# First six units' inverse as 64x64 tiles: a fused delta-rule attention and MLP kernel, with a new order

## The chip, the cores and the metric

One NeuronCore of a Trainium2 chip runs the whole kernel. The metric is device time in microseconds (us). PE is the matrix engine, DVE the vector engine, ACT the scalar engine, POOL GpSimd, and SP issues most of the DMAs.

## The reference

For 4 batches and 8 heads (32 heads in all) of 768 tokens and 48 dimensions, a delta rule runs over the tokens with a 48 x 48 state per head; its outputs, 384 wide per token, go through an MLP with the tanh form of GELU.

```python
k_n = k / (np.linalg.norm(k, axis=-1, keepdims=True) + 1e-06)
for t in range(S):
    y[:, :, t] = np.einsum('bhd,bhde->bhe', q[:, :, t], state)
    v_old = np.einsum('bhde,bhd->bhe', state, kt)
    state = state + bt[:, :, :, None] * np.einsum('bhd,bhe->bhde', kt, vt - v_old)
...
h = x @ w_in                                  # 3072 x 384 by 384 x 2048
g = 0.5 * h * (1.0 + np.tanh(c * (h + 0.044715 * h * h * h)))
return g @ w_out                              # 3072 x 2048 by 2048 x 384
```

## The kernel before, in words

The 768 tokens are cut into 12 chunks of 64. A chunk has two units (u = 2c and 2c + 1); a unit holds 16 heads as 8 pairs, with the tokens of one head of a pair on partitions 0 to 63 and of the other on 64 to 127. Within a chunk the rule is a triangular system, so each unit inverts a 64 x 64 unit triangular matrix per head, and a state is carried from chunk to chunk.

The steps of a chunk, by the names in the order text:

- k, q, v: loads (L468, mostly on SP). sq, sum, pow, eps, inv: the norms of k. kn, qb, vb: scaled k, and q and v in bf16.
- T (or Tk, Tq): transposes of k and q on PE, evicted by kT; for some units a DMA transpose, turn, takes their place. G (GD, GQ): the products k k and k q, evicted to dn and wq.
- F, lp, x0, L, and xm1, xa1 to xm6, xa6: the inverse of the 8 x 8 diagonal blocks, a recurrence on DVE for both units of the chunk together. xb: times beta. xe: spread over the blocks into zt.
- KZ, kz, GM, lw: the keys times zt, their products, and a masked copy of these into lw, which holds two 64 x 64 parts per head.
- X10, X11, then A4, rt4, B4 and A5, rt5, B5: two doubling steps of the block inverse, in the tile bd. bd is block-diagonal: 128 x 128 per pair, the two heads' 64 x 64 matrices on its diagonal and zeros elsewhere. A product's result lies 64 wide for both heads, so bringing it back into bd takes two evictions on ACT or DVE, bde0 (upper half) and bde1 (all rows, the upper ones times zero), or one eviction xi and two copies bdc0, bdc1 on POOL or DVE.
- V, K, R, U, Un, Q, O, On, S, Sn: the chunk's right-hand side, the product with bd (U), outputs (On) and the new state (Sn).
- X, xT (or turnx, a DMA transpose): the outputs turned for the MLP. up0 to up15, gelu0 to gelu3, down00 to down13, Z0, Z1, out: the MLP and its stores.

Nothing is scheduled while it runs. `ORDER` lists all steps; a step stands in the queue of the engine behind its colon (a, d, g, s for ACT, DVE, POOL, SP; PE without one), and `@` names its first PSUM bank. Each engine works through its queue in order and waits at semaphores that `Flow.emit` derives from buffers and banks. Weights come by POOL's DMA queue in four parts (w1.0, w1.1, w2.0, w2.1); `fill` steps are matmuls on zeros that nothing reads.

Of the kernel before, what the change touches and what calls it, by code (L numbers as in the profile page):

```python
# [17 lines left out]
ident:d tmplz:d tmpl0:g one:g blk1:g tmpl1:g triwq4:g pad4:d wz:d bdz5:d blk2:g ident2:g bdz4:g k0x0.11:s k0x1.10:s k0x0.10:a k0x0.00:a k0x0.01:a  # L18
k1.11:s k0x1.11:s k0x1.00:a k0x1.01:a k1.01:s k1.00:s k1.10:s beta01:a tabS:a beta00:a blk3:g pad5:d ladj5.0:d pad1:d mmlw:d bdz2:d identf:d two:d
rowz:d rows1:g mln0:g sq.0a:g triwq1:d unit:d bdz3:d ladj4.1:d own:d triwq2:d pad0:d sel:d ladj5.1:d sum.0a:d mwp0:g half:g pow.0a:a trilw2:d trilw3:d  # L20
eps.0a:d inv.0a:d mmuq:d bdz1:g sq.0b:g k2.11:s k2.10:s k2.00:s beta11:a beta10:a kn.0:g fill0@0 fill1@0 fill2@0 fill3@0 fill4@0 fill5@0 fill6@0
fill7@0 Tk.0@0 betaT0@1 sum.0b:d bdz0:d first1:d pow.0b:a eps.0b:d inv.0b:d kn.1:d Tk.1@2 sq.1:a sum.1:d kTk.0:a pow.1:a GD.0@4 kTk.1:d GD.1@2
betaT1@0 k2.01:s dn.0:a dn.1:a sq.2:a F.0@2 betaN011:d eps.1:d pad3:d betaN010:d inv.1:d pad2:d betaN000:d betaN001:d kn.2:d kn.3:d sum.2:d Tk.2@3
q0.01:s q2.00:s q0.00:s q0.10:s q0.11:s v0.00:s q2.10:s q2.11:s v0.10:s q2.01:s v0.11:s k3.10:s k3.01:s v2.10:s v0.01:s lp.0:d betaH0:d L.0@2 x0.0:d
betaL0:d xm1.0:d betaN101:d xa1.0:d betaN110:d xm2.0:d betaN100:d xa2.0:d xm3.0:d xa3.0:d betaN111:d xm4.0:d Tk.3@1 trilw1:a triwq0:a kTk.2:a GD.2@4
# [8 lines left out]
bde50.0:a bde51.0:a GM.2@2 w2.0:g pow.3:g eps.3:g xa2.2:d lw.2:d X11.2:g xm3.2:d X10.2:d xa3.2:d xm4.2:d inv.3:d xa4.2:d triwq3:d xm5.2:d xa5.2:d
xm6.2:d Tq.2@4 U.0@0 qb.3:a kTq.2:a X10.3:g X11.3:g Un.0:a GQ.2@4 Tq.3@7 kTq.3:a O.0@0 On.0:a S.0@2 A4.2@7 Sn.0:a rt4.2:d xa6.2:d X.0@0 xb.2:g xe.5:g
wq.2:d xT.0:a B4.2@7 GQ.3@2 A4.3@6 up8.0@0 up9.0 xe.4:d rt4.3:d tabG:a xi4.2:a KZ.4@4 kz.4:d B4.3@6 up10.0 up11.0 GM.4@4 wq.3:d lw.4:d X11.4:d
bde40.3:a bde41.3:a gelu2.0:a up4.0@2 up5.0 up6.0 up7.0 bdc41.2:g bdc40.2:g kn.6:g vb.3:g A5.3@0 up0.0@4 A5.2@1 up1.0 rt5.3:d vb.2:d rt5.2:d KZ.5@0
B5.3@6 gelu1.0:a sq.4:a xi5.3:a V.1@2 B5.2@1 K.1 X10.4:d kz.5:d GM.5@6 bde50.2:a R.1:a sum.4:d qb.7:g kn.7:g qb.6:g bdc51.3:g k5.00:s q4.11:s q4.01:s
q4.00:s k5.10:s q4.10:s k5.01:s q5.00:s up2.0 up3.0 A4.4@0 bdc50.3:g lw.5:d rt4.4:d turn.7:s bde51.2:a gelu0.0:a sq.5:d up12.0@2 up13.0 up14.0 U.1@6
qb.8:g B4.4@4 up15.0 down00.0@5 bde40.4:a gelu3.0:a qb.9:a Un.1:d X10.5:d pow.4:g Q.1@0 S.1@6 O.1 G.7@2 dn.7:a wqa.7:a On.1:a bde41.4:a X11.5:g  # L40
eps.4:g sum.5:d inv.4:d kn.9:d Sn.1:d kn.8:g wqb.5:g down01.0 down02.0 A4.5@2 T.9@3 turn.6:s G.6@0 X.1@6 rt4.5:d kT.9:d dn.6:a B4.5@4 T.8@7 xT.1:d
kT.8:d wq.6:d G.9@2 bde40.5:a v3.01:s v2.01:s vb.5:g vb.4:g v4.00:s q5.10:s v3.00:s q6.10:s k6.01:s q7.10:s v3.10:s k6.10:s k6.11:s v4.10:s k6.00:s
v4.01:s k7.00:s k7.01:s k7.11:s k7.10:s q6.01:s q7.11:s down03.0 bde41.5:a A5.5@4 dn.9:a wq.9:d qb.10:g Z0.0:a F.3@7 A5.4@6 V.2@0 rt5.5:d lp.3:d
rt5.4:d G.8@2 K.2 L.3@7 up12.1@4 up13.1 up14.1 B5.4@6 up15.1 dn.8:a R.2:a wqa.8:a bde50.4:a bde51.4:a F.4@2 B5.5@3 bde50.5:a bde51.5:a gelu3.1:a
x0.3:d xm1.3:d xa1.3:d xm2.3:d xa2.3:d xm3.3:d xa3.3:d xm4.3:d xa4.3:d xm5.3:d pow.5:g lp.4:d up8.1@0 up9.1 up10.1 L.4@6 up11.1 xa5.3:d xm6.3:d
eps.5:d xa6.3:d x0.4:d xb.3:g xm1.4:d xa1.4:d inv.5:d xm2.4:d xa2.4:d xm3.4:d xa3.4:d xm4.4:d xa4.4:d xm5.4:d xe.7:d xe.6:g qb.11:g U.2@2 Un.2:a
down10.0@7 down11.0 gelu2.1:a Q.2@2 S.2@4 KZ.6@0 down12.0 xa5.4:d Sn.2:d xm6.4:d xa6.4:d xb.4:d xe.9:d xe.8:d O.2 kz.6:a sq.6:a On.2:a GM.6@0 up0.1@4
up1.1 up2.1 KZ.7@6 up3.1 up4.1@2 up5.1 kz.7:a KZ.9@6 up6.1 up7.1 lw.6:d kn.11:d gelu0.1:a kz.9:d GM.7@4 lw.7:d kn.10:g wqb.8:g X11.6:g X10.6:g
gelu1.1:a turn.10:s X10.7:g X11.7:g T.11@0 KZ.8@6 down13.0 GM.9@2 G.10@4 kT.11:a G.11@0 Z1.0:d kz.8:a dn.10:a wqa.10:a dn.11:a wqa.11:a sum.6:d A4.6@7
down10.1@6 down11.1 rt4.6:d lw.9:d v3.11:s q6.11:s turnx.2:s k8.11:s k8.10:s q7.01:s A4.7@7 B4.6@4 bde40.6:a rt4.7:d vb.7:d bde41.6:d down12.1 F.5@2  # L50
lp.5:d B4.7@7 GM.8@0 A5.6@4 down00.1@5 down01.1 lw.8:d pow.6:g wqb.7:g bde40.7:a bde41.7:a vb.6:a sq.7:a q8.10:s v5.11:s k8.00:s k8.01:s v4.11:s
q7.00:s L.5@7 A5.7@0 V.3@2 rt5.6:d x0.5:d xm1.5:d B5.6@4 K.3 X10.9:g X11.9:g eps.6:d rt5.7:d xa1.5:d A4.9@0 sum.7:d wqb.11:g X10.8:g X11.8:g sq.8:g
bde50.6:a bde51.6:a R.3:a B5.7@1 bde50.7:a bde51.7:a down02.1 down13.1 down03.1 up0.2@2 xm2.5:d xa2.5:d xm3.5:d xa3.5:d rt4.9:d xm4.5:d Z1.1:d xa4.5:d
xm5.5:d Z0.1:d xa5.5:d xm6.5:d inv.6:d xa6.5:d xb.5:g U.3@0 vb.9:a Un.3:a A4.8@6 up1.2 up2.2 Q.3@4 rt4.8:d S.3@0 O.3 up3.2 up4.2@6 up5.2 up6.2 xe.11:d
Sn.3:d B4.9@0 kn.13:d On.3:a gelu0.2:a bde40.9:a bde41.9:a xe.10:g up12.2@4 B4.8@1 KZ.11@2 out11.0:s v5.01:s q6.00:s qb.13:d bde40.8:d v6.00:s
out00.0:s q8.00:s turnx.3:s up7.2 KZ.10@3 up13.2 up14.2 up15.2 A5.9@0 kz.11:a gelu1.2:a kz.10:d bde41.8:a rt5.9:d GM.10@2 GM.11@6 lw.10:d kn.12:g
pow.7:g qb.12:g X11.10:g eps.7:g lw.11:d turn.13:s vb.8:a gelu3.2:a up8.2@0 up9.2 up10.2 up11.2 up0.3@4 A5.8@2 up1.3 up2.3 up3.3 gelu2.2:a B5.9@3
X10.10:d A4.10@0 V.4@6 gelu0.3:a rt5.8:d B5.8@2 K.4 G.13@4 rt4.10:d R.4:d B4.10@0 down10.2@1 down11.2 X10.11:g wqb.10:g X11.11:g bde50.8:a bde51.8:d
turn.12:s k9.01:s sum.8:d bde50.9:a bde51.9:a dn.13:a wq.13:d inv.7:d xi4.10:d bdc40.10:g bdc41.10:g U.4@2 Un.4:a down12.2 down13.2 A4.11@2 rt4.11:d
G.12@4 Q.4@6 Z1.2:a dn.12:a S.4@0 Sn.4:d wq.12:d O.4 k9.00:s v5.10:s v5.00:s On.4:a qb.15:g k9.10:s v7.01:s v7.11:s v6.01:s k9.11:s v7.10:s q8.01:s  # L60
q8.11:s down00.2@2 F.6@3 B4.11@6 A5.10@7 up8.3@4 up9.3 lp.6:d rt5.10:d x0.6:d L.6@3 xm1.6:d xa1.6:d xm2.6:d xa2.6:d kn.15:d up10.3 down01.2 pow.8:g
# [798 lines left out]
```

## Time and profile before

| | |
|---|---|
| median of 3 runs | 263.66 us (261.0 to 264.15) |
| the profiled execution | 262.76 us, its span 261.0 us |
| mean granted PE clock | 0.928 |
| busy: PE, DVE, ACT, POOL | 236.6, 191.2, 169.5, 135.7 us |
| MLP matmuls | 576 (L780) and 384 (L791) |
| product matmuls of the inverse (L660) | 768 |

The span runs from the first to the last instruction. Busy times are unions of an engine's instructions; an engine that is busy is not always at its peak. The granted clock is the share of full speed that PE was given.

### The profile page before, as it was taken

The numbers are of one execution on the slowest core, as the hardware profiler recorded it, in microseconds if no ns is written. First come the engines' busy times: TensorE is split into PE (matmuls) and PEld (weight loads), VectorE is DVE, ScalarE is ACT, GpSimd is POOL, SyncE is SP. The second block draws the span as 40 slices with busy tenths as digits, with TensorE's granted clock in tenths as the row PEclk, the third lists the DMA queues.
The fourth block names the chain that finished last, engine by engine and source line by source line (L and its number), as shares of the span: only waits on it lengthen the run. The fifth ranks groups of instructions, "written<-read, shape, count | busy, mean of one in ns | idle before, by whom it ended". The sixth has DMA issues, their size and how long they took to land.

```text
span 261.0 us, 11939 instructions
## 1 busy us (share of the span) xinstructions
PE 236.6 (91%) x5320; PEld 182.3 (70%) x5320; DVE 191.2 (73%) x444; ACT 169.5 (65%) x261; POOL 135.7 (52%) x172
## 2 busy tenths in 40 slices
PE   5188688976999999999999998999999999999994
...
PEclk9655755699999999999999999999999999999999
...
GB/s 97 162 173 197 123 148 199 127 128 141 133 114 144 124 153 57 122 125 110 162 119 140 108 36 118 159 37 135 130 76 3 4 154 32 31 36 48 45 93 60
DMA packets 104019, 28.10 MB, mean 108 GB/s; under 512 B 98080, under 2 KB 103200, under 8 KB 103968
## 3 DMA queue, kind: packets, MB, share of 16 engines
q1 hardware_dynamic: 98736, 23.56, 51.4%
...
## 4 chain that ended last, share of the span: by engine, by line
PE 62%; DVE 12%; DMA 10%; SPq 6%; POOL 4%; ACT 3%; issue 2%; POOLq 0%
PE ps L780 20%; PE ps L791 20%; DMA qraw<-in_q_dram 8%; SPq L468 6%; PE ps L660 6%; DVE lw L600 2%; PE ps L597 2%; PE ps L586 2%; PE ps L708 2%; PE ps L546 2%; DMA kraw<-in_k_dram 2%; PE ps L610 1%; PE ps L729 1%; PE ps L522 1%; PE ps L715 1%
## 5 line engine op out<-in xcount | busy, mean ns | idle before, releaser
L780 PE MATMUL ps<-xT,W 128*128 128x256 bf16 x576 | 75.6, 274 | 1.6 <-issue 0.8
L791 PE MATMUL ps<-W,gT 128*128 128x384 bf16 x384 | 72.3, 326 | 0.0
L784 ACT ACTIVATE gT<-ps 128x1024 bf16<-128x1024 f32 x48 | 48.3, 1020 | 22.0 <-PE ps L780 21.7
L780 PEld LDWEIGHTS ps<-xT,W 128*128 128x128 bf16 x576 | 51.7, 98 | 10.7 <-issue 1.2
L791 PEld LDWEIGHTS ps<-W,gT 128*128 128x128 bf16 x384 | 34.1, 97 | 18.6
L678 POOL COPY bd<-xi 64x256 f32<-64x256 f32 x28 | 11.0, 398 | 49.3 <-ACT xi L341 43.5
L600 DVE CAST_PREDICATED lw<-mlw,ps 128x1024 bf16<-128x1024 uint16 x24 | 29.1, 1218 | 7.6 <-PE ps L597 7.4
L650 POOL TENSOR_SCALAR_AFFINE_SELECT bd<-lw 64x512 bf16<-64x512 bf16 x33 | 22.3, 678 | 21.4 <-DVE lw L600 16.0
L494 POOL TENSOR_TENSOR nrm<-nrm,half 128x16 f32<-128x16 f32 x10 | 29.4, 2943 | 4.5 <-DVE nrm L492 4.3
L666 DVE TENSOR_TENSOR rl<-ps,two 128x384 bf16<-128x384 f32 (+1 forms) x48 | 22.8, 486 | 10.6 <-PE ps L660 10.4
L660 PE MATMUL ps<-rl,bd 128*128 128x64 bf16 x384 | 19.5, 198 | 0.7 <-DVE rl L666 0.7
L344 ACT ACTIVATE bd<-ps,low 128x512 bf16<-128x512 f32 x27 | 18.3, 677 | 2.3 <-DVE bd L341 2.3
L341 ACT ACTIVATE bd<-ps 64x512 bf16<-64x512 f32 x27 | 15.7, 585 | 5.9 <-PE ps L660 5.7
L632 DVE TENSOR_TENSOR ps<-ps,xl 128x96 f32<-128x96 f32 (+2 forms) x72 | 16.0, 223 | 4.0 <-PE ps L626 2.1
L660 PEld LDWEIGHTS ps<-rl,bd 128*128 128x128 bf16 x384 | 16.4, 101 | 3.1 <-DVE rl L666 0.9
L522 PE MATMUL ps<-ident,tok 128*128 128x128 bf16 x96 | 10.1, 256 | 8.9 <-POOL tok L513 6.7
L341 DVE COPY ob<-ps 128x384 f32<-128x384 f32 x7 | 3.9, 551 | 19.0 <-PE ps L791 19.0
L660 PEld LDWEIGHTS ps<-lw,bd 128*128 128x128 bf16 x384 | 15.1, 98 | 3.7 <-ACT bd L344 0.5
L635 DVE TENSOR_TENSOR xl<-ps,xl 128x96 bf16<-128x96 f32 (+2 forms) x72 | 16.2, 225 | 1.8
L660 PE MATMUL ps<-lw,bd 128*128 128x32 bf16 (+1 forms) x384 | 17.1, 183 | 0.3 <-ACT bd L344 0.3
L513 POOL TENSOR_TENSOR tok<-kraw,nrm 128x384 bf16<-128x384 f32 x16 | 14.6, 914 | 3.3 <-DVE xl L635 1.1
L341 ACT ACTIVATE dn<-ps 128x512 bf16<-128x512 f32 x20 | 11.9, 594 | 5.7 <-PE ps L546 5.5
...
## 6 DMA issues: line engine op xcount, KB each, us to landing
...
W<-in_moe_w_in_dram POOLq DMA_DIRECT2D x2, 768.0 KB, 10.5
W<-in_moe_w_out_dram POOLq DMA_DIRECT2D x2, 768.0 KB, 10.8
...
kT<-tok SPq DMA_TRANSPOSE x12, 3.3
```

What stands on the lines that cost most here:

```text
L341: return e.activation(out, in_, ACT.Copy) if e is nc.scalar else e.tensor_copy(out, in_)
L344: return e.activation(out, in_, ACT.Copy, scale=by) if e is nc.scalar else e.tensor_scalar(out, in_, by, None, op0=ALU.mult)
L494: if e is nc.scalar else e.tensor_tensor(nr[:, 1, hx], nr[:, 0, hx], half[:, hx], ALU.pow), reads=[nrn, "half"] + ["one"] * (c < ROOTS),
L600: A(("dve",), op("lw"), lambda e, P: e.copy_predicated(lw[m][:, :, :, :].rearrange("p h w t -> p h (w t)"), mlw[:, :, :].rearrange("p w t ...
L632: A(("dve",), f"xm{m}.{c}", lambda e, P, m=m, w=w, part=part: e.tensor_tensor(part(P), P(f"L.{c}")[:, off[m]:off[m] + 2 * H * w].rearrange ...
L635: A(("dve",), f"xa{m}.{c}", lambda e, P, m=m, part=part: e.tensor_tensor(xl[y][:, :, m + 1:LB], part(P), xl[y][:, :, m + 1:LB], ALU.add), ...
L650: A(("pool", "dve"), op(f"X1{a}"), lambda e, P, src=lw[m][hf(a), :, 1, :], dst=bd[b_][hf(a), :, hf(a)], a=a: e.affine_select(out=dst, in_= ...
L660: ins = e.matmul(P(name)[:, C * h + c0:C * h + c1], bd[b_][:, h, :], rhs[:, h, c0:c1])
L666: A(("dve",), op(f"rt{i}"), lambda e, P, i=i, c0=c0, c1=c1, r_=r_: e.tensor_tensor(r_[:, :, c0:c1], P(ps(f"A{i}")).rearrange("p (h t) -> p ...
L780: ins = e.matmul(P(ph)[:, 256 * f:256 * f + 256].rearrange("p (x t) -> p x t", x=2), W1[:, j, 128 * (i + f):128 * (i + f) + 128], x_[:, :, ...
L784: A(("act",), f"gelu{i // 4}.{c}", lambda e, P, i=i, ph=ph: e.activation(g_[:, i:i + 4, :], P(ph).rearrange("p (f t) -> p f t", f=4), ACT. ...
L791: ins = e.matmul(P(po)[:, 0:DM], g_[:, f, 128 * b:128 * b + 128], W2[:, f, :], start=(f == 0), stop=(f == FC - 1))
```

## The change

For the first six units (`TU = 6`, chunks 0 to 2) bd is no longer block-diagonal. It holds each head's 64 x 64 matrix in columns 0 to 63 of its own 64 partitions, and a product is two matmuls of 64 x 64 per pair, each in its quarter of the array. One eviction, be4 or be5, brings all of a product back; X1 is one operation where X10 and X11 were two; U takes 32 matmuls per chunk instead of 16. The zeroing of a bd tile (bdz) now stands ahead of units 6 to 11, the first that need it.

For all units lw keeps 112 columns per head instead of 128, written from column 8 on, and GM's matmuls are 48 and 56 wide instead of 64.

By choice of the order text, two units of a chunk can share one operation: knc for kn, qbc for qb, vbc for vb, xec for xe. The order uses knc 6, qbc 7, vbc 9 and xec 9 times. A second form of the leaf recurrence (Lc, ym, ya) is added and not used. `rows` is copied from the identity (rows2) instead of being selected. Three chunks' square roots are on ACT instead of two (`ROOTS`).

The order text is new throughout. It has 20 `fill` steps instead of 8; chunks 0 and 1 alternate at the start, with the loads of k0's second half and k1 first; w2.0 and w2.1 stand behind X1.3 and X1.5 on POOL. Six units are transposed by T instead of eight and 14 by turn; X is used three times instead of two.

The diff, cut to its core:

```diff
-    ROOTS = 2
+    ROOTS = 3
+    TU = 6
+    LW = 2 * C - 16
...
-        lw = sb("lw", [128, H, 2, C], BF16, NN)
+        lw = sb("lw", [128, H, LW], BF16, NN)
...
-            if s < NB:
+            if TU <= s < NB:
                 A(("dve", "pool"), f"bdz{s}", ...)
...
-            for i in range(70):
+            for i in range(140):
                 n = f"fill{i}"
...
+            if not x:
+                A(("dve", "pool"), f"xec.{c}", lambda e, P: e.tensor_tensor(
+                    zts[:, H * m:H * (m + 2), :].rearrange("p h (b j) -> p h b j", j=LB), ...
...
-                    for y, z, w in ((2, 0, 0), (0, 2, 1)):
+                    for y, z, o, c0, c1 in ((2, 0, C, 0, LW - C), (0, 2, 0, LB, C)):
                         for p, a in quad:
...
+            if TU <= u - NB + TU < 2 * TU and u >= NB:
+                A(("dve", "pool"), f"bdz{b_}", lambda e, P: e.memset(bd[b_][:, :, :].bitcast(F32), 0.0), writes=bds)
+            if u < TU:
+                xd = bd[b_][:, :, 0:C]
+                A(("dve", "pool"), op("X1"), lambda e, P: e.tensor_tensor(xd, lw[m][:, :, 0:C], two[:, :].unsqueeze(1).to_broadcast([128, H, C]), ALU.add),
+                  reads=[f"lw{m}", "two"], writes=bds)
-            for a in range(2):
+            for a in range(2 if u >= TU else 0):
                 A(("pool", "dve"), op(f"X1{a}"), ...)
...
                     for h in range(H):
+                        for a in range(2 if u < TU else 0):
+                            ins = e.matmul(P(name)[hf(a), C * h + c0:C * h + c1], bd[b_][hf(a), h, 0:C], rhs[hf(a), h, c0:c1])
+                        if u < TU:
+                            continue
                         ins = e.matmul(P(name)[:, C * h + c0:C * h + c1], bd[b_][:, h, :], rhs[:, h, c0:c1])
...
+                if u < TU:
+                    A(EV, op(f"be{i}"), lambda e, P, i=i: copy(e, bd[b_][:, :, 0:C], P(ps(f"B{i}")).rearrange("p (h t) -> p h t", h=H)), frees=[ps(f"B{i}")], writes=bds)
+                    continue
...
+                        for a in range(2 if us_[x] < TU else 0):
+                            ins = e.matmul(P(ps("U"))[hf(a), o:o + D], bd[us_[x] % NB][hf(a), 4 * p + g, 0:C], rb[hf(a), p, x, g, :])
```

The new order from the inverse of chunk 0 to the first `up`:

```
X1.3:g be4.0:d A5.1@7 V.0@2 xm3.2:d v1.11:s rt5.1:d xa3.2:d xm4.2:d v1.00:s A4.3@1 R.0:a xa4.2:d xm5.2:d k3.10:s xa5.2:d xm6.2:d
A5.0@2 xa6.2:d B5.1@0 k4.01:s xb.2:g rt5.0:d GQ.3@4 wqb.1:g rt4.2:d B5.0@3 v2.11:s rt4.3:d be5.0:a q3.01:s be5.1:d tabG:a B4.3@3 xec.2:d k5.10:s U.0@6
q3.10:s wq.3:d sq.3:g KZ.5@2 k4.00:s Un.0:a bdz0:d k4.10:s O.0@6 KZ.4@4 w2.0:g k4.11:s sum.3:d On.0:a fill92@5 vbc.1:a B4.2@5 kz.4:d X.0@6 pow.3:g
be4.3:d GM.4@0 be4.2:d xT.0:a lw.4:d S.0@4 kz.5:a up4.0@6
```

More of the change, by code (lines that the diff above doesn't have):

```diff
@@ L17 @@
 ORDER = """
[L18 to L25, printed above, removed]
@@ L34 @@
[L34 to L41, printed above, removed]
@@ L42 @@
[L42 to L61, printed above, removed]
```

248 lines of the change are left out of this document (157 added, 91 removed).

## The prediction

> **What bounds the kernel now.** I read the page first, then busy time by windows, then TensorE's (PE's) timeline around each gap, and last the groups of instructions by line.
>
> ```profile
> span 261.0 us, 11939 instructions
> PE 236.6 (91%) x5320; PEld 182.3 (70%) x5320; DVE 191.2 (73%) x444; ACT 169.5 (65%) x261; POOL 135.7 (52%) x172
> PE   5188688976999999999999998999999999999994
> PEclk9655755699999999999999999999999999999999
> ```
>
> PE is busy 91% of the span, so no other engine bounds the whole. But the two last rows split the span: in the first eight of forty slices PE has gaps and its granted clock is near half; after that it is full. Columns of the next view are the window, its length, busy time of PE, PEld, DVE, ACT and POOL with counts, granted clock, DMA share and GB/s.
>
> ```profile
> 10.00:15.00 5.00, 2.78 (x47) 2.06 (x48) 4.69 (x18) 2.80 (x6) 3.58 (x6) 0.50 1.26 164
> ...
> 55.00:60.00 5.00, 3.42 (x117) 3.01 (x113) 3.60 (x6) 3.70 (x6) 2.54 (x5) 1.00 0.70 128
> 60.00:65.00 5.00, 3.03 (x138) 2.42 (x138) 2.73 (x5) 2.19 (x4) 4.14 (x3) 1.00 0.97 138
> ...
> 70.00:100.00 30.00, 30.00 (x816) 23.49 (x815) 28.30 (x77) 23.77 (x38) 21.57 (x20) 1.00 0.72 126
> ...
> 130.00:160.00 30.00, 28.47 (x584) 21.03 (x580) 23.98 (x58) 18.60 (x29) 11.84 (x17) 1.00 0.53 99
> ```
>
> Early, DVE is the full engine (4.69 of 5). Between 55 and 65 PE loses 3.55 us, in 130 to 160 another 1.5. From 70 to 100 PE is full, with DVE close behind at 28.3 of 30.
>
> ```profile
> 43.89 0.82 PE L729 MATMUL ps<-rs,bd 128*128 128x48 bf16 x16
> 49.10 1.12 PE L780 MATMUL ps<-xT,W 128*128 128x256 bf16 x6
> 57.77 0.62 PE L597 MATMUL ps<-kT 48*64 48x64 bf16 x32 [1.58 <-ACT xi L341]
> 64.28 0.44 PE L738 MATMUL ps<-us,tok 64*64 64x48 bf16 x32 [1.97 <-DVE us L341]
> 252.18 5.36 PE L791 MATMUL ps<-W,gT 128*128 128x384 bf16 x32
> ```
>
> The first MLP matmul starts at 49.10; the last ends at 252.18 + 5.36 = 257.54. So 261.0 = 49.1 before the first MLP step + 208.4 of filled PE + 3.5 of last copy and store. In the 208.4 lie 1.58 + 1.97 + 1.5 = 5.1 of visible gaps, which leaves 203.3 of PE work. A change shows only if it moves the 49.1, the 203.3 or the 5.1. The execution itself took 262.76 us, 1.76 more than its span, and lies 0.9 under the median of 263.66.
>
> **The PE work after the first MLP step.** I count the steps behind the first `up` in both orders. KZ goes from 20 to 18, GM from 20 to 19, B4 from 21 to 20, T from 6 to 4 (two more go by DMA), X from 1 to 2, one filler is added; all MLP steps are the same. Prices are start to start.
>
> ```profile
> 66.90 0.61 PE L522 MATMUL ps<-ident,tok 128*128 128x128 bf16 x8
> 67.45 0.42 PE L546 MATMUL ps<-kT 48*64 48x128 bf16 x16
> ...
> 77.67 0.44 PE L708 MATMUL ps<-st,kT 48*64 48x48 bf16 x32
> 77.95 0.47 PE L738 MATMUL ps<-us,tok 64*64 64x48 bf16 x32
> 78.35 0.41 PE L586 MATMUL ps<-zt,tok 128*64 128x128 bf16 x8
> 78.70 0.82 PE L791 MATMUL ps<-W,gT 128*128 128x384 bf16 x4
> ...
> 88.08 0.36 PE L660 MATMUL ps<-lw,bd 128*128 128x48 bf16 x8
> 88.28 0.39 PE L660 MATMUL ps<-rl,bd 128*128 128x64 bf16 x8
> 88.51 0.81 PE L791 MATMUL ps<-W,gT 128*128 128x384 bf16 x4
> ```
>
> A T is 0.55 (66.90 to 67.45), an X six eighths of it, 0.41; KZ 0.35; GM, 32 small tiles like L708, 0.28; B4 0.23. Saved: 0.70 + 0.28 + 0.23 + 1.10 - 0.41 - about 0.2 for the filler = 1.7. Against it stand changes between whole-array and 64-row tiles: L708 followed by another tiled step takes 0.28, L738 followed by another shape 0.40, so a change costs about 0.1. The new order has 130 of them behind the first `up` where the old has 109: 21 x 0.1 = 2.1 lost. Net +0.4; from both sides, -1.7 (changes free) to +2.
>
> The 64x64 products are not in the trace. Step A4 is now 8 matmuls in 0.20, B4 8 in 0.23; each becomes 16 in two of four quarters. L708 sends 32 through four quarters in 0.28: eight rounds of 35 ns. Two quarters need eight rounds too: 0.14 if the rate of instructions is the limit, 0.28 if each quarter is. I take equal; all 24 products differ by -2.0 to +1.9 us, most of it ahead of the first `up`, where PE is not the limit.
>
> [...]
>
> **The first MLP step.** Before, chunk 0 goes ahead of chunk 1. Now chunks 0 and 1 go side by side (GD.1, GD.3, GD.2, GD.0, then F.1, F.0 and two interleaved leaf recurrences), and the parts differ as follows.
>
> ```profile
> 0.81 3.70 ACTq L468 DMA_DIRECT2D kraw<-in_k_dram  x5
> 5.20 1.28 ACT L364 ACT_TABLE_LOAD   x1 [5.20 <-issue]
> ...
> 42.08 0.68 DVE L553 CAST_PREDICATED wq<-muq,ps 128x512 bf16<-128x512 uint16 x1
> 42.68 0.23 DVE L635 TENSOR_TENSOR xl<-ps,xl 128x80 bf16<-128x80 f32 x1
> ```
> ```profile
> L600 DVE CAST_PREDICATED lw<-mlw,ps 128x1024 bf16<-128x1024 uint16 x24 | 29.1, 1218 | 7.6 <-PE ps L597 7.4
> L666 DVE TENSOR_TENSOR rl<-ps,two 128x384 bf16<-128x384 f32 (+1 forms) x48 | 22.8, 486 | 10.6 <-PE ps L660 10.4
> L650 POOL TENSOR_SCALAR_AFFINE_SELECT bd<-lw 64x512 bf16<-64x512 bf16 x33 | 22.3, 678 | 21.4 <-DVE lw L600 16.0 <-DVE ps L632 2.6 <-POOL bd L650 0.5
> L344 ACT ACTIVATE bd<-ps,low 128x512 bf16<-128x512 f32 x27 | 18.3, 677 | 2.3 <-DVE bd L341 2.3
> L341 ACT ACTIVATE bd<-ps 64x512 bf16<-64x512 f32 x27 | 15.7, 585 | 5.9 <-PE ps L660 5.7
> L632 DVE TENSOR_TENSOR ps<-ps,xl 128x96 f32<-128x96 f32 (+2 forms) x72 | 16.0, 223 | 4.0 <-PE ps L626 2.1
> L579 DVE TENSOR_TENSOR zt<-xb,blk 128x1024 bf16<-128x1024 bf16 x17 | 14.2, 847 | 1.1 <-POOL xb L637 0.8
> L341 ACT ACTIVATE dn<-ps 128x512 bf16<-128x512 f32 x20 | 11.9, 594 | 5.7 <-PE ps L546 5.5
> L568 POOL TENSOR_TENSOR wq<-wq,muq 128x512 bf16<-128x512 bf16 x10 | 11.5, 1154 | 0.2
> ```
>
> Each eviction of a product for the first six units falls from 585 + 677 = 1262 ns on ACT to one operation of the 594 form: 0.67 us shorter, twice per unit. X1 on POOL falls from 2 x 678 to one of the L568 form, 1154. lw shrinks from 1024 to 832 elements, by proportion 990 ns, and I take 1.02. Two units' scaling in one saves only a start each. pow.2 moves from POOL to ACT, beside pow.0 and pow.1. The zeroing of six bd tiles moves from the start behind these units' last use, half of it on DVE, inside the gap term below. On SP's queue q1 now goes ahead of v0, so the tok casts stop waiting for it; I give that no worth of its own, since DVE's list is longer than the loads.
>
> ACT sets the start. Its list up to dn.2 has 10 DMA issues at 0.74 (3.70 / 5), 2 table loads at 1.28, six evictions and two presets of the 0.594 form, and about 4.7 of a wide preset, squares and small operations (an estimate from their sizes): 19.4 us from 0.8, so 20.2. Some issues run beside a table load, as one did at 5.20, and F.1 follows dn.2, so I put lp.1 at 20 (17.5 if all issues but the first hide, 22 if loads come late). From lp.1 to be5.1 DVE's list is 36 leaf operations at 0.223 (8.0), four lw (4.1), four wq at 0.68 (2.7), six rt at 0.486 (2.9), two xe (1.7), two be and a kz at 0.68 (2.0), and lp, x0, xb, ladj (about 2.8): 24.2 end to end. But the operation after the wq at 42.08 starts 0.08 before its recorded end, and about 60 operations, many now independent of the last, could save up to 4.8: 19.4 to 24.2. I take 22, a middle, since both chains alternate. be5.1 then ends at 42. From U.0 to the first `up` the old kernel needs 49.10 - 43.89 = 5.2, and that path keeps its operations: first `up` at 47.2, between 42 and 51.
>
> **The gaps.** At 57.77 GM.5 came late; now KZ.5 and GM.4 lie ahead of the first `up` and GM.5 right behind it. At 64.28 S.1 waited for Un.1, which DVE held behind sq.5; both are on ACT now. So 3.55 goes. New is B5.3, about 1 us: rt5.3 stands on DVE behind lw.4, lw.5 and qbc.3, and up7 to K.1 queue behind B5.3. The 1.5 I keep, and add 1.3 for a new order on a DVE that stays close behind PE (28.3 of 30), though lw's 0.2 x 24 eases it. Together 3.8 (2 to 12: the 2 if B5.3 alone remains, the 12 if DVE's list from 70 on overruns PE as it did from 55 to 65).
>
> **Sum.** 47.2 + 203.3 + 0.4 + 3.8 + 3.5 = 258.2 span, + 1.76 = 260.0, 1.1% under the profiled 262.76 and 1.4% under the median.
>
> **Rivals.** *W2 late (slower).*
>
> ```profile
> 32.09 1.00 POOL L479 DMA_DIRECT2D W<-in_moe_w_out_dram  x1
> ...
> 36.87 0.94 POOL L479 DMA_DIRECT2D W<-in_moe_w_out_dram  x1
> ```
> ```profile
> W<-in_moe_w_out_dram POOLq DMA_DIRECT2D x2, 768.0 KB, 10.8
> L494 POOL TENSOR_TENSOR nrm<-nrm,half 128x16 f32<-128x16 f32 x10 | 29.4, 2943 | 4.5 <-DVE nrm L492 4.3
> ```
>
> w2.0 now stands on POOL behind X1.0 to X1.3, xb.2, wqb.1 and sq.3, w2.1 behind pow.3 (2.9) and X1.5 besides: about 43 and 50, landing 10.8 later at 54 and 61. PE wants them at down00.0 (about 59) and down02.0 (about 63). Slack is 2 us; past that PE stops one for one. Landing at 70 costs 7: 267.0. For it, POOL is in order and waits on DVE; against it, its list is shorter. 0.15.
>
> *Clock (faster).* 20 fillers instead of 8, eight of them just ahead of Tk.1, hold the full clock through the start; At 1.00 instead of 0.50 PE's steps there halve. The first `up` comes at 44 and gaps shrink to 2: 44 + 203.3 + 0.4 + 2 + 3.5 + 1.76 = 255.0. Against it, the fillers cover only some gaps, and DVE's list stays. 0.25. [...]
>
> *Early gain lost.* ACT and DVE wait for each other, first `up` at 49.5, gaps as before at 5.1: 49.5 + 203.3 + 0.4 + 5.1 + 3.5 + 1.76 = 263.6. That the shorter evictions shorten nothing, since DVE's list and not the products sets U.0, is this case; for it, DVE was full early before as well. 0.20.
>
> The forecast has 0.40. The range, 253.5 to 267.0, leaves out the far ends of both outer cases. A measurement of this kernel can tell about 2% from no change: under 258.4 is faster (the clock case and a third of the forecast: 0.36), over 268.9 slower (part of the W2 case and of the lost gain: 0.13), the rest 0.51.
>
> **What would show it.** Right: the first MLP matmul near 47, no PE gap over 1.5 us between 55 and 65, be evictions near 600 ns, lw near 1.0 us, PE full from 70 on. Wrong: the first `up` past 50; a gap ahead of down00 or down02 released by DMA; more than 3 us of gaps between 70 and 220.

## The result and the profile after

The changed kernel takes 265.57 us (265.14 to 266.0, 4 runs) where the kernel before took 262.45 (261.0 to 264.15, 4 runs) beside it: a ratio of 1.0131, 95% interval 1.0082 to 1.0179. Measured once more later (`after_again` below) the ratio was 1.0082 (1.0054 to 1.0110). Ratios compare undisturbed runs alone, so they are not quite the quotients of the medians. The kernel is slower by about 1%, within the 2% that were counted as no change, and inside the range; the forecast was 1.1 to 1.4% on the other side. The profiled execution took 265.38 us, its span 263.5.

The page of the changed kernel, the rows that answer to those of before:

```profile
span 263.5 us, 12329 instructions
PE 241.7 (92%) x5562; PEld 183.5 (70%) x5562; DVE 186.0 (71%) x428; ACT 163.3 (62%) x248; POOL 117.1 (44%) x147
PE   0877797599899999999999999999999999999994
PEclk9999755759999999999999999999999999999999
```

DVE, ACT and POOL all have less to do than before (191.2, 169.5 and 135.7 us), and the kernel is slower. The clock row shows two dips, and the second, in the ninth slice, was not there before. Busy time by windows (columns as in the prediction):

```profile
50.00:55.00 5.00, 2.57 (x75) 2.10 (x75) 1.80 (x3) 1.09 (x2) 0.63 (x3) 0.79 0.21 32
55.00:60.00 5.00, 5.00 (x52) 3.16 (x50) 4.07 (x7) 1.53 (x2) 3.70 (x3) 0.53 0.41 39
60.00:65.00 5.00, 4.79 (x141) 3.63 (x141) 1.91 (x4) 3.33 (x5) 0.00 (x0) 1.00 1.32 180
...
70.00:100.00 30.00, 29.77 (x772) 22.50 (x762) 24.81 (x67) 21.62 (x34) 14.69 (x18) 1.00 0.66 117
...
130.00:160.00 30.00, 29.94 (x665) 23.57 (x654) 23.15 (x55) 18.87 (x26) 17.98 (x20) 1.00 0.75 129
```

The gaps of before, between 55 and 65 and in 130 to 160, are gone. But from 50 to 55 PE is busy for 2.57 of 5 us and every other engine for less, and from 55 to 60 PE is busy all the time at a clock of 0.53: 52 matmuls where before there were 117. PE's timeline shows the place:

```profile
43.37 1.03 PE L778 MATMUL ps<-rs,bd 64*64 64x48 bf16 x32
45.32 0.64 PE L612 MATMUL ps<-zt,tok 128*64 128x128 bf16 x8 [0.92 <-DVE zt L602]
...
49.32 0.45 PE L789 MATMUL ps<-us,tok 64*64 64x48 bf16 x25
52.43 0.24 PE L789 MATMUL ps<-us,tok 64*64 64x48 bf16 x7 [2.66 <-issue]
52.61 0.55 PE L831 MATMUL ps<-xT,W 128*128 128x256 bf16 x3
...
255.27 4.71 PE L842 MATMUL ps<-W,gT 128*128 128x384 bf16 x28
```

U.0 starts at 43.37, about where it did (43.89). S.0 is one step of 32 matmuls that waits for nothing inside; after 25 of them PE stands 2.66 us, "issue" as its releaser: the profile shows nothing that it waited for. The first `up` then comes at 52.61, 3.5 later than before and 5.4 later than forecast. The last matmul ends at 259.98, 2.4 later than before.

The 2.4 divide as follows. From the first `up` to the end of the last matmul, I take off the time in which no matmul runs and half of the time at a granted clock of 0.50 (an `up` matmul takes 0.23 us there, from 56.24 on, and 0.12 at 1.00, from 64.61 on); what is left is PE's work at full clock. The times at which the clock changes are read from the trace.

| | first up | to the last matmul's end | no matmul | at 0.50 | work left |
|---|---|---|---|---|---|
| before | 49.10 | 208.44 | 5.90 | 0.65 | 202.2 |
| changed | 52.61 | 207.38 | 1.29 | 6.83 | 202.7 |

3.5 us more before the first `up`, 3.1 of clock and 0.5 of work, against 4.6 us of gaps saved.

### The profile page after: what moved, and what is told of

It reads as the page before. It is cut to its first block, busy times and chain, and to the rows that moved or that the text cites. A ratio compares the mean times of both kernels' runs of the same rounds, so it can differ in the third digit from the quotient of the medians.

```text
span 263.5 us, 12329 instructions
## 1 busy us (share of the span) xinstructions
PE 241.7 (92%) x5562; PEld 183.5 (70%) x5562; DVE 186.0 (71%) x428; ACT 163.3 (62%) x248; POOL 117.1 (44%) x147
## 4 chain that ended last, share of the span: by engine, by line
PE 81%; DVE 10%; ACT 4%; issue 2%; POOL 2%; ACTq 0%; POOLq 0%
PE ps L831 25%; PE ps L842 24%; PE ps L705 6%; PE ps L623 3%; PE ps L612 3%; PE ps L756 3%; PE ps L702 2%; PE ps L567 2%; PE ps L636 2%; PE ps L763 2%; PE ps L780 2%; PE ps L789 1%; PE ps L802 1%; DVE zt L605 1%; ACT gT L835 1%
## 5 line engine op out<-in xcount | busy, mean ns | idle before, releaser
L842 PEld LDWEIGHTS ps<-W,gT 128*128 128x128 bf16 x384 | 34.2, 97 | 18.6 <-ACT gT L835 0.2
L626 DVE CAST_PREDICATED lw<-mlw,ps 128x832 bf16<-128x832 uint16 x24 | 24.4, 1019 | 7.5 <-PE ps L623 7.4
L344 ACT ACTIVATE bd<-ps 64x512 bf16<-64x512 f32 (+1 forms) x24 | 14.2, 590 | 16.0 <-PE ps L702 12.6
L344 ACT ACTIVATE ob<-ps 128x384 f32<-128x384 f32 x19 | 9.4, 492 | 16.9 <-PE ps L842 16.9
L658 DVE TENSOR_TENSOR ps<-ps,xl 128x96 f32<-128x96 f32 (+4 forms) x72 | 15.4, 222 | 2.4 <-PE ps L652 0.9
L661 DVE TENSOR_TENSOR xl<-ps,xl 128x96 bf16<-128x96 f32 (+4 forms) x72 | 15.7, 226 | 1.4
L350 ACT ACTIVATE kT<-ps 128x512 bf16<-128x512 f32 x17 | 9.9, 596 | 9.0 <-PE ps L612 9.0
L574 DVE CAST_PREDICATED wq<-muq,ps 128x512 bf16<-128x512 uint16 x17 | 11.4, 683 | 4.6 <-ACT dn L344 4.5
L612 PE MATMUL ps<-zt,tok 128*64 128x128 bf16 x192 | 10.6, 240 | 3.3 <-DVE zt L605 2.3
L705 PE MATMUL ps<-lw,bd 128*128 128x48 bf16 (+1 forms) x288 | 12.8, 180 | 0.0
L500 DVE TENSOR_REDUCE nrm<-sq 128x16 f32<-128x768 f32 (+1 forms) x13 | 11.4, 879 | 1.7 <-POOL sq L499 1.4
```

The lines of the kernel that those rows point to most:

```text
L344: return e.activation(out, in_, ACT.Copy) if e is nc.scalar else e.tensor_copy(out, in_)
L612: ins = e.matmul(P(ps("KZ"))[hf(p), 128 * g:128 * g + 128], tok[s][:, 0, 2 * g + p, :], zt[m][:, 4 * p + g, :])
L626: A(("dve",), op("lw"), lambda e, P: e.copy_predicated(lw[m][:, :, LB:LW], mlw[:, :, :].rearrange("p w t -> p (w t)")[:, LB:LW].bitcast(U1 ...
L658: A(("dve",), f"xm{m}.{c}", lambda e, P, m=m, w=w, part=part: e.tensor_tensor(part(P), P(f"L.{c}")[:, off[m]:off[m] + 2 * H * w].rearrange ...
L661: A(("dve",), f"xa{m}.{c}", lambda e, P, m=m, part=part: e.tensor_tensor(xl[y][:, :, m + 1:LB], part(P), xl[y][:, :, m + 1:LB], ALU.add), ...
L705: ins = e.matmul(P(name)[:, C * h + c0:C * h + c1], bd[b_][:, h, :], rhs[:, h, c0:c1])
```

## The experiments

**Why PE stands in S.0.** Theories: *Supply* (PE has no instruction to run), *Tiles* (the 64x64 matmuls are slow) and *Order* (DVE's and ACT's new lists are late). The first hint is in the DMA queues: q8, of kind "instruction", moves 43 packets and 0.70 MB, 16 KB each, and PE has 5562 matmuls and 5562 weight loads: about 63 bytes per instruction, one packet per 259 of them (the count further down gives 256). Packet times below are read from the trace.

`w2_later`, one word of the order text:

```
- ... k4.10:s O.0@6 KZ.4@4 w2.0:g k4.11:s ... V.1@4 eps.3:g A5.2@0 ...
+ ... k4.10:s O.0@6 KZ.4@4 k4.11:s      ... V.1@4 eps.3:g w2.0:g A5.2@0 ...
```

> The changed kernel with one word moved: w2.0 (the first half of W2) is issued on POOL behind eps.3, at about 48 to 51 instead of 44.1. Supply: the block that S.0 needs is fetched by 48, S.0 runs through, first up at 49.5 to 50.5, the clock stays at 1.00 from 49.5 on, 262 to 263 us. Order and Tiles: the pause of 2.7 us stays, first up 52 to 53, 265 to 266 us. If W2 is then late instead: down00.0 waits for a DMA.

Measured: 263.74 us, ratio to before 1.0064 (1.0031 to 1.0097). PE's timeline of `w2_later`, and then the DMA queues from 46.0 to 49.5, the changed kernel's row first and `w2_later`'s second:

```profile
49.36 0.49 PE L789 MATMUL ps<-us,tok 64*64 64x48 bf16 x32
49.89 0.50 PE L831 MATMUL ps<-xT,W 128*128 128x256 bf16 x3
```
```profile
q0 software_dynamic: 681, 0.52, 114.2%
```
```profile
q8 instruction: 1, 0.02, 2.4%
```

S.0 runs through its 32 matmuls and the first `up` comes at 49.89. In the changed kernel W2's packets take 114% of the 16 engines' time in that stretch, so they overlap, and no instruction packet moves; its packet begins at 49.97, after PE has stopped, and PE resumes 2.46 later. With W2 moved, it begins at 46.55. The clock then stays at 1.00 from 49.6 on. Supply holds, although its 262 to 263 us was missed by 0.7. In `after_again` the pause is there again (2.32 us, packet at 49.40).

> The changed kernel itself once more, beside the next three on the same chip, since 1.8 us are to be told apart. All theories: 265 to 266 us, a pause of 2 to 3 us without a semaphore in or near S.0, first up at 52 to 53.

Measured: 266.2 us, 1.0082 (1.0054 to 1.0110), first `up` at 51.85. Against this second figure the move of w2.0 is worth less: its ratio lies 0.2 to 0.7% below the two of the changed kernel, and the intervals overlap, so a gain in time is likely but not shown. In the profiles the last matmul ends 1.7 to 2.1 us earlier.

`e9_shift` leaves W2 alone and adds instructions:

```
+ A(PE, f"small{i}", ...)   # three steps of 20 matmuls, 64x64 zeros by 8 columns
- ... KZ.2@3 dn.4:a xe.1:g KZ.0@2 ...
+ ... KZ.2@3 dn.4:a xe.1:g small0@2 small1@2 small2@2 KZ.0@2 ...
```

> The changed kernel with 60 small matmuls of zeros (64x64 by 8 columns, no part of the result) ahead of KZ.0, where TensorE waits 2.1 us for xe.0: 120 more TensorE instructions, w2.0 where it is. Supply (a block of 256 instructions falls due when TensorE gets through the one before; the one due at 46.5 is held up behind w2.0's transfer, 45.8 to 52.0): it now falls due some 2.5 us earlier, ahead of the transfer, and is begun by 45; S.0 runs through, first up at 49.5 to 51, 263 to 264.5 us, faster than the changed kernel although it does more. If W2's transfer hurts in another way than through the instructions, or the pause belongs to S.0: the pause stays in S.0, first up 52.5, 265.5 us or more.

Measured: 268.24 us, 1.0150 (1.0114 to 1.0187). S.0 runs through (53.50 to 54.04), as Supply said; but its time is missed by 4 us, for the most part because a pause now stands in GM.1, which Supply did not foresee. There w1.1 was moving, whose packets end at 34.1. The rows below are the pauses of `e9_shift`, and of `old_order` and `no_fill`, which come further down.

```profile
35.93 0.31 PE L631 MATMUL ps<-kT 48*64 48x48 bf16 x5 [2.85 <-issue]
```
```profile
49.97 0.35 PE L703 MATMUL ps<-lw,bd 64*64 64x48 bf16 x5 [2.72 <-issue]
```
```profile
52.63 0.53 PE L622 MATMUL ps<-kT 48*64 48x48 bf16 x24 [1.80 <-issue]
```

Three different steps, each cut in its middle: the pause belongs to no step. In these three traces and the two of the changed kernel PE resumes 2.2 to 3.0 us after an instruction packet begins (32.93, 47.17 and 50.44 here), and POOL's weights were moving when it began or had landed 0.5 us before.

What the pauses have in common shows when PE's instructions (matmuls, weight loads and semaphore steps) are counted in order of their start. Over all 18 traces 24 pauses of 0.5 us or more have the releaser "issue". Every one stands behind an instruction whose number leaves 193 on division by 256: 961 in `e9_shift`, 1473 in `old_order`, 1729 in the changed kernel (both times) and in `no_fill`. (In `old_form` and `w2_later` the count gives 187, and six matmul records are missing there.) So PE stops at the border of a block of 256 instructions, whatever step that border falls into. In the changed kernel's trace each of the 43 packets begins behind a border of its own, 0.1 to 4.7 us after PE has passed it (median 1.4). The packet that ended the pause at 1729 began 4.7 us after PE had entered the block before that border in the changed kernel, 4.6 in `after_again` and 4.3 in `no_fill`; in `w2_later` the one ahead of the same border began after 1.2.

**What the tile form is worth.** Form and order, each alone, and each with w2.0 out of the way.

`old_form` is the changed order with `TU = 0`: X1 as X10 and X11, be as bde0 and bde1, the bdz at the start.

> The changed kernel's order with the block-diagonal products, X10/X11 and two evictions per product for all units (the tile form alone undone). Theory Supply (in the changed kernel TensorE has no instruction to run from 49.8 to 52.4, in the middle of S.0, because the 16 KB block that it needs is fetched only at 49.97, while w2.0's transfer fills the DMA engines from 46 to 50.5; the pause then sends the clock back to 0.5 for 6.8 us): about 110 fewer TensorE instructions stand ahead of S.0, so the block falls due at another place and S.0 need not stall; first up near 50.5, 263 us. Rival Tiles (the doubled 64x64 matmuls themselves are what is slow): first up 50 or earlier and 262 us or less. Rival Order (the new DVE and ACT lists are late whatever the form): the four evictions on the way cost some 2.6 us more, first up 53 to 55, 266 to 268 us.

Measured: 264.96 us, 1.0117 (1.0078 to 1.0156); U.0 at 44.58, first `up` at 51.49. S.0 waits 1.29 for the eviction of B4.2 on DVE (bd), not for instructions:

```profile
51.12 0.44 PE L790 MATMUL ps<-us,tok 64*64 64x48 bf16 x32 [1.29 <-DVE bd L348]
```

Tiles is refuted (without them it is no faster), and Order's 266 too. Supply's 263 was missed by 2 us as well: without the pause, the wait for a longer eviction takes part of its place.

`old_order` puts the changed code into the order of before: one X1, be4, be5 at the place of each pair, bdz ahead of units 6 to 11.

> The changed kernel's code (64x64 tiles and whole evictions for the first six units, the narrow lw) put into the order of before (the form alone done; the zeroing of bd for units 6 to 11 stands ahead of their X10/X11). Order: the form costs nothing or saves, 260 to 262.5 us, first up 47 to 49. Tiles: the slower and more numerous matmuls show here too, 264 to 266 us. Supply: depends on where a block falls due against w2.0 and w2.1; a pause of 1.5 us or more without a semaphore between 45 and 65 would speak for it, none would leave 261 to 262.5 us.

Measured: 266.94 us, 1.0184 (1.0138 to 1.0231). U.0 at 43.92 as before; then the pause of 2.72 shown above, first `up` at 52.20. That is the sign that Supply had named; Order's 260 to 262.5 us is refuted.

`old_form` and `old_order` with w2.0 later (behind eps.3, behind X1.3):

> old_form with w2.0 issued behind eps.3, as in w2_later. Supply: in old_form no TensorE pause ahead of the first up came without a semaphore, so moving w2.0 brings little: 264 to 265.3 us, and with W2 out of the way in both, the tile form is worth what lies between this and w2_later (263.74): 0.5 to 1.5 us gained by the form. If old_form gains as much as the changed kernel did (1.8 us), W2's place costs something other than the instruction supply: 263.2 us or less.

> old_order with w2.0 issued on POOL behind X1.3 (about 46 instead of 36.3; w2.1, which goes first in that order, stays at 31). Supply: the block that fell due at 44.9 and was begun at 47.17, behind 33.5 to 46.7 of W2, is begun by 45.5; the pause of 2.95 from 47.0 goes, first up 49.5 instead of 52.2, 264 to 265 us (266.94 less 2 to 3). Tiles: the pause stays somewhere, 266 to 267.5.

Measured: `e8_old_form_w2` 265.52 us, 1.0115 (1.0079 to 1.0150), nothing gained, as Supply said; `e7_old_order_w2` 266.19 us, 1.0115 (1.0068 to 1.0162), the pause down to 0.42 and the first `up` at 49.69 instead of 52.20. The pause went as Supply said; the time is the one that Tiles had named (266 to 267.5), since PE's work stayed long. The table of above for these kernels:

| | first up | to the last matmul's end | no matmul | at 0.50 | work left |
|---|---|---|---|---|---|
| w2_later (new order, tiles) | 49.89 | 207.99 | 4.57 | 0 | 203.4 |
| e8_old_form_w2 (new order, old form) | 52.02 | 208.27 | 4.19 | 3.69 | 202.2 |
| e7_old_order_w2 (old order, tiles) | 49.69 | 210.44 | 3.64 | 3.32 | 205.1 |
| two_units (below) | 49.19 | 208.34 | 4.17 | 3.54 | 202.4 |

Tiles bring the first `up` forward by 2.1 us in the new order and add 1.2 us of PE work behind it; in the old order, where more of the six units lie behind the first `up`, they add 2.9 to the 202.2 of before. The single steps show it, at full clock, start to start (U.1 and two A4 of the changed kernel, then a U of before, each with the step that follows; the A4 of before is in the prediction):

```profile
62.65 0.69 PE L778 MATMUL ps<-rs,bd 64*64 64x48 bf16 x32
63.27 0.62 PE L543 MATMUL ps<-ident,tok 128*128 128x128 bf16 x8
...
72.22 0.68 PE L702 MATMUL ps<-lw,bd 64*64 64x32 bf16 x32
72.83 0.51 PE L814 MATMUL ps<-ident,xo 128*128 128x128 bf16 x6
```
```profile
75.88 0.56 PE L729 MATMUL ps<-rs,bd 128*128 128x48 bf16 x16
76.28 1.46 PE L791 MATMUL ps<-W,gT 128*128 128x384 bf16 x8
```

A U is 0.62 against 0.40, an A4 0.305 against the 0.20 of the prediction.

So `two_units` takes tiles for units 0 and 1 alone, on `w2_later` (`TU = 2`; units 2 to 5 as in `old_form`, with xi and POOL copies for be4.2, be4.3, be5.4).

> w2_later with 64x64 tiles for units 0 and 1 alone; units 2 to 5 have the block-diagonal form again (two evictions on ACT, or one and two POOL copies for be4.2, be4.3 and be5.4). Tiles (behind the first up TensorE sets the time, and there a product of 16 tiles takes 0.30 to 0.36 against 0.20 to 0.24 for eight 128-wide steps, a U 0.62 against 0.40): 12 products and 2 U behind the first up save 1.5 to 2 us, first up within 0.5 of 49.9, 261.5 to 262.3 us. Rival (TensorE waits for the longer evictions instead): what is saved is lost to waits on ACT bd or POOL bd between 50 and 75, 263.5 us or more.

Measured: 264.06 us, 1.0031 (0.9997 to 1.0065). The work is 1.0 us less than in `w2_later`; part is lost again to a wait for POOL's copy (1.14, at 52.06). It is level with the kernel before and not faster; the 261.5 to 262.3 of Tiles was missed, and the rival's 263.5 or more held. Against `e8_old_form_w2` the gain lies outside both intervals: tiles pay for the units ahead of the first `up` (three evictions of units 2 to 4, xi and copies here, differ besides).

**Does the clock set the early part?** `no_fill` drops the 20 fillers from the order; `more_fill` adds 39 to `w2_later`, nine ahead of KZ.0 and one ahead of each PE step from GM.2 to X.0.

> The changed kernel without its 20 fillers (512-column matmuls of zeros, no part of the result). If the early full clock that they hold (1.00 from 12 to 29) is worth something, the first F and L come later, lp.1 at 20 or later, first up 53.5 or later, 266.5 us or more. If DVE and ACT set the time up to U.0 (Order), lp.1 stays within 0.5 of 18.9 and U.0 within 0.7 of 43.4. Supply: 40 instructions fewer ahead of S.0 move the block's due time about 1 us earlier against w2.0's transfer, so the pause in S.0 shrinks or moves: 263 to 265.5 us.

Measured: 266.77 us, 1.0178 (1.0135 to 1.0222). U.0 at 44.09, lp.1 at 19.24; the pause of 1.80 lies behind the first `up`, and the clock is at 0.50 from 38.6 to 59.1 and from 72.8 to 76.2. (The profiled execution, with 269.46 us, was the longest.) Order's reading of the early part held; the time came out above Supply's.

> w2_later with 39 more fillers (zeros, no part of the result): nine ahead of KZ.0, in the 2.1 us in which TensorE waits for xe.0, and one ahead of each TensorE step from GM.2 to X.0. Clock (the pause at 25.6 drops the clock to 0.50 from 29 to 49.6): with the pause filled the clock stays at 1.00 past 29, steps on the way of 0.64 take 0.3, first up at 46.5 to 48, 260.5 to 262 us. Rival (DVE sets the time up to U.0 at any clock, and fillers stand in the way): U.0 stays within 0.7 of 43.4, first up 49 to 50.5, 263.5 us or more; if the clock falls all the same, fillers at 0.43 each make it 265 us or more.

Measured: 266.84 us, 1.0143 (1.0093 to 1.0194). Windows of `more_fill`:

```profile
25.00:29.00 4.00, 3.62 (x63) 1.82 (x59) 4.00 (x5) 1.79 (x3) 3.98 (x3) 1.00 1.29 186
29.00:33.00 4.00, 4.00 (x111) 2.48 (x110) 3.32 (x5) 1.91 (x4) 1.94 (x3) 1.00 1.16 209
41.00:45.00 4.00, 3.68 (x90) 1.99 (x85) 3.79 (x12) 1.41 (x2) 2.45 (x3) 1.00 0.58 106
```

The clock holds at 1.00 from 12 us to the end, and U.0 still comes at 45.74, 2.3 later than in `w2_later`, the first `up` at 50.91: fillers of 385 ns stand in the way, and DVE is as full (4.00 of 4 in the first row). A full clock bought in this way does not bring the first `up` forward. The runs of the kernel before beside these experiments say the same without any edit: in 25 of them the mean granted clock was 0.98 or more, so nearly all of the start ran at full clock, and in 47 it was at most 0.935; their medians are 263.2 and 262.7 us.

**The way to the first up.** `chain` straightens what lies between U.0 and the first `up` of `w2_later`; `two_units_chain` does it on `two_units`, with B4.2 and GM.4 behind the second `up` and without the filler.

```
- ... B4.3 xec.2 U.0 wq.3 KZ.5 Un.0 O.0 KZ.4 On.0 fill92 vbc.1 B4.2 X.0 GM.4 xT.0 S.0 up4.0 ...
+ ... B4.3 wq.3 xec.2 U.0 Un.0 O.0 On.0 S.0 KZ.5 X.0 KZ.4 fill92 B4.2 xT.0 up4.0 vbc.1 up5.0 GM.4 ...
```

> w2_later with the way from U.0 to the first up put in a straight line: wq.3 ahead of xec.2 on DVE, O.0 and S.0 ahead of KZ.5 and KZ.4, X.0 ahead of KZ.4, vbc.1 behind xT.0 on ACT, GM.4 behind the second up. Order (0.92 waited for xec.2, 0.6 of KZ.4, 0.5 of B4.2 and 0.8 of vbc.1 stand in that way): first up at 48.4 to 48.8 instead of 49.9, 262.3 to 262.8 us. If what the first up gains is lost behind it (units 4 and 5 are later by the moved steps; first down 62.96 in w2_later), the time stays at 263.7.

> two_units with the straight way from U.0 to the first up of chain, and B4.2 and GM.4 behind the second up. In chain KZ.4, a filler and B4.2 stood ahead of the first up, 1.7 us: without the last two first up at 48.5 to 49.3, 260.5 to 261.7 us. If the steps put behind (units 2, 4 and 5) are then missed between 55 and 75: 262 us or more.

Measured: 265.2 us, 1.0058 (1.0019 to 1.0098), S.0 2.7 us earlier at 46.67 and the first `up` at 50.21 (48.4 to 48.8 expected), behind KZ.4, the filler and B4.2; and 264.48 us, 1.0041 (1.0012 to 1.0069), first `up` at 48.98, not faster than `two_units` although earlier.

The scaling: operations on the zt tile, the changed kernel first, then `both_on_dve`, which takes xec.0 and xec.1 on DVE for the four xe and puts units 0 and 1 ahead of 2 and 3 in KZ, GM and lw (`two_units_dve`: the same on `two_units`, and be4.3 as two evictions on DVE; `two_units_best`: KZ.5 behind O.0, vbc.1 behind xT.0 besides). Durations are minimum, median and maximum in ns.

```profile
L605 DVE TENSOR_TENSOR zt<-xb,blk x2: 686/1543/2400, 24.7 to 25.3; 128x1024 bf16<-128x1024 bf16 x2
L605 POOL TENSOR_TENSOR zt<-xb,blk x2: 1952/2151/2350, 25.2 to 27.1; 128x1024 bf16<-128x1024 bf16 x2
```
```profile
L602 DVE TENSOR_TENSOR zt<-xb,blk x3: 1218/1226/2384, 25.1 to 43.2; 128x2048 bf16<-128x2048 bf16 x3
```

> w2_later with the scaling of units 0 to 3 as xec.0 and xec.1 on DVE, none on POOL, and KZ, GM and lw of units 0 and 1 ahead of those of 2 and 3. Theory Port (DVE's xe.0 takes 2.40 instead of 0.69 while POOL runs xe.1, and xec.2 2.29 instead of 1.22 while POOL runs sq.3: the two engines hold each other up): with POOL idle the two xec take 1.2 each, all four units are scaled at 27.2 instead of 29.5, lw.1 ends at 31 instead of 34.2, U.0 starts at 41 to 42.5 instead of 43.4, first up 48 to 49.3, 262 to 263.3 us. Rival (TensorE at half clock sets the way, or DVE's list behind lp.2): lw.1 earlier, U.0 still 43 or later, 263.5 to 264.5 us. If xec takes 2.2 or more with POOL idle, Port falls.

> two_units with the same edit, and be4.3 as two evictions on DVE instead of one and two POOL copies (A4.3's bd came 1.1 us late from POOL in two_units). Port: first up 48 to 49, behind it as two_units, 261 to 262.5 us. Rival: 263 to 264.5 us.

> two_units_dve with KZ.5 behind O.0 (it waits 0.9 to 1.3 us for xec.2 in front of O.0) and vbc.1 behind xT.0. If these steps are on the way: first up 0.8 to 1.5 us ahead of two_units_dve, 260 to 261.5 us, level with or below the kernel before. If what the first up gains is lost behind it, as in chain: the time of two_units_dve.

Measured: xec takes 1.22 with POOL idle, 2.38 beside it, and a single xe 0.69 against 2.40: Port holds. But the way gained nothing: lw.1 ended at 30.6 instead of 34.2, and U.0 came at 43.62, the first `up` at 50.21. `both_on_dve` 265.12 us, 1.0105 (1.0070 to 1.0140); `two_units_dve` 263.62, 1.0054 (1.0026 to 1.0081); `two_units_best` 264.21, 1.0060 (1.0031 to 1.0089), with the first `up` at 50.84 and 51.01 in the last two, later than in `two_units`. The rivals of all three held.

`leaf_later` (on `two_units_dve`) lets units 0 and 1 through first:

```
  DVE, changed:    ... lw.3 xa2.2 be4.0 xm3.2 rt5.1 xa3.2 ... xa6.2 rt5.0 rt4.2 rt4.3 be5.1 xec.2 (U.0)
  DVE, leaf_later: ... rt4.0 lp.2 rt4.1 lw.2 rt5.0 x0.2 rt5.1 xm1.2 xa1.2 be5.1 (U.0) lw.3 xm2.2 ... xa6.2 rt4.2 rt4.3
```

> two_units_dve with DVE's and TensorE's lists put so that units 0 and 1 go first: the leaf steps of chunk 2 from xm2.2 to xa6.2, rt4.2 and rt4.3, lw.3 (2.1, 0.9 and 1.0 us of DVE, all ahead of be5.1 in the changed kernel) behind be5.1 or beside it, A4.0, A4.1, B4, A5, B5 of units 0 and 1 as soon as their lw is there, O.0, S.0 and X.0 straight behind U.0. Theory List (the new order put units 2 and 3 on DVE in front of U.0): U.0 at 37 to 39.5 instead of 43.4 to 43.9, first up 43 to 45.5. What of it reaches the end then shows: if the first up sets the end, 257 to 259.5 us; if the units 2 to 5, now later, are missed behind it (U.1 at 61 to 63 as before), TensorE stands 4 to 6 us between 50 and 65, 261 to 263.5 us. Rival (half clock or DMA holds U.0): U.0 41 or later, 263 us or more.

Measured: 269.1 us, 1.0232 (1.0195 to 1.0270). PE's timeline of `leaf_later`:

```profile
40.95 1.05 PE L778 MATMUL ps<-rs,bd 64*64 64x48 bf16 x32 [0.37 <-DVE bd L344]
...
47.41 0.82 PE L831 MATMUL ps<-xT,W 128*128 128x256 bf16 x3 [0.48 <-ACT xT L344]
...
52.86 0.43 PE L567 MATMUL ps<-kT 48*64 48x64 bf16 x16 [2.63 <-DVE xi L344]
...
57.71 0.41 PE L705 MATMUL ps<-rl,bd 128*128 128x64 bf16 x8 [1.05 <-DVE rl L711]
...
60.44 0.41 PE L705 MATMUL ps<-rl,bd 128*128 128x64 bf16 x8 [0.97 <-DVE rl L711]
...
71.61 0.42 PE L567 MATMUL ps<-kT 48*64 48x128 bf16 x16 [1.88 <-DMA kT<-tok]
```

U.0 comes 2.4 us earlier than in the changed kernel, short of List's range and just ahead of the rival's, and the first `up` at 47.41. Yet the kernel is the slowest of all: PE waits for the eviction of B4.2, for rt5.3 and rt5.2 and for a turned k, 10.0 us without a matmul behind the first `up` and 8.9 at half clock, and W2, issued later by the same move, ends only at 70.5. What was put behind the first `up` is missed there.

## Why the prediction was wrong

- **The step that failed: "From U.0 to the first `up` the old kernel needs 5.2, and that path keeps its operations: first `up` at 47.2."** It measured 9.24. 2.7 are the pause in S.0, for which the sum had no term; `w2_later` takes it out and leaves 6.5. Of the other 1.3, 0.92 are the wait of KZ.5, which stands in front of O.0, for xec.2 (2.28 us on DVE beside POOL's sq.3, where an xec of `both_on_dve` takes 1.22 with POOL idle), and 0.14 a longer U.0 (32 tiles). The steps of other units on the way cost 2.7 as in the order before. The path kept its operations, but the order put one into PE's queue whose input was not ready, and PE's instructions were not supplied.
- **DVE's list from lp.1 to be5.1.** lp.1 started at 18.92 (forecast 20, right); be5.1 ended at 43.06 instead of 42, so the list took 24.1, not 22. "Two xe (1.7)" measured 3.0, since POOL scales at the same time: that term was mis-sized by 1.3. Of the 24.2 end to end plus this, 1.4 came off where I had 2.2, net of 1.3 in which DVE waits for PE. The rows of the two xe, of be5.1 and of xec.2:

```profile
24.71 3.00 DVE L605 TENSOR_TENSOR zt<-xb,blk 128x1024 bf16<-128x1024 bf16 x2
...
42.38 0.68 DVE L344 CAST bd<-ps 128x512 bf16<-128x512 f32 x1
42.98 2.28 DVE L602 TENSOR_TENSOR zt<-xb,blk 128x2048 bf16<-128x2048 bf16 x1
```

- **Together** 1.4 + 4.0 = 5.4, all of the error of the sum: from the first `up` to the last matmul's end the forecast had 203.3 + 0.4 + 3.8 = 207.5, and 207.38 were measured. But its parts were wrong both ways: no matmul for 1.3 instead of 3.8, and 3.4 lost to a clock for which the sum had no term. That the two came out even is luck. The pause caused the loss of clock: it had risen to 1.00 at 49.5 and fell again at 52.9, for 6.8 us, and without the pause, in `w2_later`, it did not fall.
- **"First `up` + work" as a sum.** A first `up` near 47.2 does not bring the time by itself: `leaf_later` has 47.41 and 269.1 us, and `two_units_chain` has an earlier one than `two_units` and no better time. The first `up` sets the end only while the second chunk is ready behind it.
- **Small prices.** lw 1.02, be 0.6 and a tail of 3.5 held; X1 on POOL took 1203 ns instead of 1154. Of 64x64 products I took "equal" between 0.14 and 0.28 for 16 matmuls: 0.305 to 0.35 were measured, 19 to 22 ns a matmul in two quarters, where L708 of the kernel before puts 32 through four quarters in 0.28, under 9 ns each. My 0.20 was an estimate from L708 alone. The 3.55 of gaps between 55 and 65 did go.
- **The rivals.** *Early gain lost* (first `up` 49.5, 263.6 us) is what the kernel does without the pause: 49.89 and 263.74. *W2 late* saw the right transfer and the wrong damage: no row of PE between 49 and 70 waits for a DMA, but its traffic, as the moves of w2.0 let one infer, held up PE's instructions. *Clock*: the clock stood at 1.00 from 12 to 29, and with 39 more fillers from 12 to the end, and neither brought the first `up` forward (52.61 and 50.91). That the 20 fillers hold it is not shown: without them, in `no_fill`, a KZ took 0.41 at 28.04 and 0.64 at 30.48, in the changed kernel 0.64 at 45.32, where the clock is 0.50.

```profile
L626 DVE CAST_PREDICATED lw<-mlw,ps 128x832 bf16<-128x832 uint16 x24 | 24.4, 1019 | 7.5 <-PE ps L623 7.4
L344 ACT ACTIVATE bd<-ps 128x512 bf16<-128x512 f32 x7 | 4.2, 598 | 12.6 <-PE ps L702 12.6
L688 POOL TENSOR_TENSOR bd<-lw,two 128x512 bf16<-128x512 bf16 x5 | 6.0, 1203 | 9.1 <-DVE lw L626 9.1
```

The sign named for a wrong forecast, a first `up` past 50, came.

Moving W2 takes away this pause and not the kind. PE still stands for "issue" at 67.36 in `w2_later`, and at 71.81 in `no_fill`:

```profile
67.36 0.27 PE L802 MATMUL ps<-us,wq 64*64 64x48 bf16 x9 [1.77 <-issue]
```
```profile
71.81 0.22 PE L701 MATMUL ps<-rl,bd 64*64 64x64 bf16 x2 [1.84 <-issue]
```

Both stand at the same border (2497, six records short in the first), and the packets began at 64.33 and 68.66, 1.4 and 5.7 us after W2's last (62.9 and 63.0). PE resumes 3.0 and 3.2 us after them. What held these two up is open. That the packet at 49.97 waits in a queue behind W2 is inferred from its start and from the two moves, not seen. No version beat the kernel before; `two_units` is level with it.
